# A fused attention and feed-forward kernel: one matmul chunk of the head moved, and the last store cut into two partition halves

## The chip, the cores and the metric

The kernel runs on one core of one Trainium2 chip. The metric is the device time of one execution in microseconds, as the median of repeated runs. A core has five engines that run their own instruction streams and meet at semaphores: TensorE (PE) multiplies matrices into PSUM, VectorE (DVE), ScalarE (ACT) and GpSimd (POOL) work elementwise, and SyncE (SP) issues transfers. ACT issues a few transfers too. The transfers of all of them run on the core's 16 DMA engines; in the profile, SP's queue is q1 and ACT's is q10.

## The reference

Input x is 2048 tokens of 448 features, bf16. All of it is computed on the normalised tokens:

```python
xn = layernorm(x)
# A: linear attention with 16 heads of 28 features, no softmax
q, k, v = heads(xn @ wqkv)
pq, pk = phi(q), phi(k)          # phi(t) = where(t > 0, t + 1, exp(t)) + 1e-6
kv, z = sum_s(pk * v), sum_s(pk) # per head: 28 x 28 and 28
s = merge(pq @ kv / (pq @ z + 1e-6)) @ wo
# B: feed-forward with squared ReLU, 1792 hidden features
g = silu(relu(xn @ w1 + b1) ** 2 @ w2 + b2)
out = x + s * g
```

## The kernel before, in words

The tokens stand as 16 tiles of 128, in four groups of four. The 448 features are three chunks of 128 rows and a rest of 64; the rest is held twice, in both partition halves, so that two matmuls on 64 rows each can run in the two halves of the PE array.

The kernel lists its operations in program order. A small planner (`Program.schedule`, line 89) then places them: the order on PE and SP is the order in which they are written; on ACT, DVE and POOL the planner picks by its own estimated durations and due times, and some operations may go to either of two engines. PSUM has eight banks; each new accumulator gets the bank that comes free first in the plan. For the head, the orders on ACT and DVE are written out by hand (line 1125 on). `emit` (line 232) turns the plan into instructions and waits; the last thing on SP is a wait until every store to the output has landed.

The stages, in order of PE's work:

1. The head (lines 1062 to 1146). While the first tiles load, PE runs eight warm-up matmuls. Then tiles 0 to 3 are normalised on DVE (`ln_norm`, line 486; its 1/std comes from two ACT operations, lines 477 and 481), transposed by PE against an identity matrix (`turn`, line 523), and copied back as xT by DVE or ACT. Between the transposes PE runs what already has its operands: `k0` and `k1` are the key projections of tiles 0 and 1 (line 647, 512 columns per chunk), `first[0..3]` are the first 256 columns of the hidden features h0 to h3 for tiles 0 and 1 (line 694, 256 columns per chunk). `h_mains(fi, ks)` (line 1088) issues the chunks `ks` of h`fi`; `h_mains(1)` is all three. A chunk of h0 or h1 reads the first w1 piece, a load of 192 KB, and chunk c of xT of tiles 0 and 1. `turn("T..")` names: T00 to T02 are chunks 0 to 2 of tile 0, T10 and T12 those of tile 1, T03 the rests of tiles 0 and 1, T2 and T3 the chunks of tiles 2 and 3, T23 their rests. The operation at line 1106 transposes the bias b1.
2. The streams (lines 1159 to 1187): keys, queries and hidden features of all four groups, four accumulators at a time. The transposed tiles 4 to 15 come from DMA transposes that SP issues. The hidden features 8 to 13 read the last third of w1 (`w1c`, line 464), which SP loads in three transfers.
3. Token sums, the denominator, the folding of wv and wo, and then the gates and the outputs (lines 1192 to 1233): gates `gg` are 14 matmuls over the hidden features (line 969) and a Silu on ACT; outputs `ss` are four matmuls (line 1037), a product with the gate on DVE, the residual add, and a store issued by SP.
4. The end (lines 1234 to 1243). Tile 15 goes in two column pieces, `ca` with 288 and `cb` with 160 columns. The gate of `cb` has its bias added by a matmul (line 968), so that ACT reads PSUM directly; DVE multiplies and adds the residual; the store of `ca` is issued by SP and that of `cb` by ACT.

The order of PE's instructions around the first place of the change is therefore: T00, T01, T02, k0 chunk 0, T10, k0 chunk 1, T12, k0 chunk 2, k1 chunk 0, h0 chunk 0, k1 chunks 1 and 2, b1, h0 chunks 1 and 2, T03, h1 chunks 0 to 2, T2, h2, T3, h3, T23, and then the rests.

Of the kernel before, what the change touches and what calls it, by code (L numbers as in the profile page):

```python
# [9 lines left out]
P = 128  # L10
S, D, F = 2048, 448, 1792
# [45 lines left out]
class Program:  # L57
# [8 lines left out]
    def add(self, eng, emit, reads=(), writes=(), dur=0.2, alts=(), nbytes=0):  # L66
        op = Op(eng, emit, reads, writes, dur, alts, nbytes)
        for t in op.reads:
            w = self.writer.get(t)
            if w is not None:  # L70
                op.raw.add(w)
            self.readers.setdefault(t, []).append(op)
        for t in op.writes:
            w = self.writer.get(t)
            if w is not None and w is not op:
                op.deps.add(w)
            for r in self.readers.get(t, ()):
                if r is not op:
                    op.deps.add(r)
            self.writer[t] = op  # L80
            self.readers[t] = [r for r in self.readers.get(t, ()) if r is op]
        op.raw.discard(op)
        op.deps |= op.raw
        for d in op.deps:
            d.succ.append(op)
        self.ops.append(op)
        return op
# [203 lines left out]
def bass_recurrent_scan__linear_attn_block__dense_activation_squared_relu__prompt_kernel(  # L291
# [4 lines left out]
    with ExitStack() as es:  # L296
# [44 lines left out]
        obuf = xn[:, :, :].rearrange("p s d -> p (s d)")[:, 0 : 8 * D].rearrange("p (s d) -> p s d", d=D)  # L341
# [12 lines left out]
        def bcast(ap, reps):  # L354
# [9 lines left out]
                out=ident[:, :], in_=ident[:, :], pattern=[[-1, P]], compare_op=ALU.not_equal, fill=1.0,  # L364
# [37 lines left out]
        o_r = out[0].rearrange("(p s) d -> p s d", s=NT)  # L402

        def dma(eng, dst, src, writes, nbytes, reads=()):
            return add(eng, lambda e, _: e.dma_start(dst, src), reads, writes, 0.5, nbytes=nbytes)
# [117 lines left out]
        def turn(name, si, chunks, eng, tiles=1):  # L523


            b = Buf("T")
            pieces = [(si + t, c) for t in range(tiles) for c in chunks]
            n = len(pieces)
            for i, (t, c) in enumerate(pieces):
                reads = xn_of(t)[min(c, 1) :][:1] or xn_of(t) if c < 3 else [("xd", t)]  # L530
                add(
                    "pe",
                    lambda e, _, i=i, t=t, c=c: e.transpose(  # L533
                        ps(b)[:, i * 64 : (i + 1) * 64].bitcast(bf), xn[:, t, c * P : (c + 1) * P], ident[:, :]
                    ),
                    reads + ["ident"] + ([b] if i else []), [b], 0.06,
                )

            def ev(e, _):
                src = ps(b)[:, 0 : n * 64].bitcast(bf)  # L540
                dst = xT[:, chunks[0], si * P : (si + tiles) * P]
                if len(chunks) > 1:
                    src = src.rearrange("p (c k) -> p c k", c=n)
                    dst = xT[:, chunks[0] : chunks[0] + n, si * P : (si + 1) * P]
                if eng == "dve":
                    return e.tensor_copy(dst, src)
                return e.activation(out=dst, in_=src, func=AF.Copy)

            dur = 0.06 + 0.09 * n if eng == "dve" else 0.16 + 0.11 * n
            head[name] = add(eng, ev, [b], [("xT", t, c) for t, c in pieces], dur)  # L550
# [51 lines left out]
        def mains(u, ks=K3, reads=None):  # L602


            def f(e, _):
                for k in ks:
                    last = u.mm(e, 2, k, k == 0, False)
                return last

            reads = u.reads if reads is None else reads  # L610
            add("pe", f, reads + ([u.bank] if ks[0] else []), [u.bank], len(ks) * MM(u.n))
# [376 lines left out]
        def full(u, ks=range(NF), more=[]):  # L988


            ks = list(ks)

            def f(e, _):
                for i, k in enumerate(ks):
                    last = u.mm(e, 2, k, i == 0, i == len(ks) - 1)
                return last

            add("pe", f, u.reads + more, [u.bank], len(ks) * MM(u.n))
            u.out()
# [17 lines left out]
                [("o", si % 8, c.start), ("x", si)], [("o", si % 8, c.start)], 1.1 if eng == "pool" else 0.35, alts=alts,  # L1017
            )

        def store(si, c=slice(0, D), eng="sp"):  # L1020
            dma(
                eng, o_r[:, si, c], obuf[:, si % 8, c], [("out", si, c.start)], P * (c.stop - c.start) * 2,
                [("o", si % 8, c.start)],
            )

        def ss(si, c=slice(0, D), alts=(), eng="pool", end=True):
            b = Buf("S")
            n = c.stop - c.start
            tok = slice(si * P, (si + 1) * P)
            rtok = slice(si // 2 * P, (si // 2 + 1) * P)  # L1030

            def mm(e, h, k, start, stop):
                if k < 3:
                    q, m = pqT[half[h], k, tok], msb[half[h], k, c]
                else:
                    q, m = pqR[half[h], rtok], msz[:, si % 2, c] if h == 2 else msb[half[h], 3, c]
                return e.matmul(ps(b)[:, 0:n], q, m, start=start, stop=stop)  # L1037

            def out():
                finish(si, b, c)  # L1040
                residual(si, c, eng, alts)
                if end:
                    store(si)

            return Acc(b, reads_s(si), mm, out, n)
# [42 lines left out]
        def h_mains(fi, ks=K3):  # L1088
            xs = xT_of(0) + xT_of(1)
            mains(first[fi], ks, [x for x in xs if x[2] in ks] + [("w1a", fi // 2 * 3)])  # L1090
# [9 lines left out]
        mains(k0, (2,), [("xT", 0, 2)])  # L1100
        mains(k1, (0,), [("xT", 1, 0)] + wk0)
        h_mains(0, (0,))
        mains(k1, (1, 2), [("xT", 1, 1)])
        bb = Buf("B1")
        b1v = lambda: ps(bb)[:, 0 : P // 2].bitcast(bf)
# [3 lines left out]
        )  # L1109
        h_mains(0, (1, 2))  # L1110
        turn("xT03", 0, (3,), "act", 2)
        h_mains(1)
        turn("xT2", 2, K3, "act")
        h_mains(2)
        turn("xT3", 3, K3, "dve")
# [20 lines left out]
        a, b, c, d = second  # L1136
# [99 lines left out]
        ca, cb = slice(0, 288), slice(288, D)  # L1236
        full(ss(14), KS, ["msz"])
        full(gg(15, ca))
        full(ss(15, ca, eng="dve", end=False), KS, ["msz"])
        store(15, ca)  # L1240
        full(gg(15, cb, True), range(NF + 1))
        full(ss(15, cb, eng="dve", end=False), KS, ["msz"])
        store(15, cb, "act")
        pr.schedule()
        pr.emit(nc, es)

# [27 lines left out]
```

## Time and profile before

| | |
|---|---|
| median of 16 runs | 141.27 us (140.74 to 141.93) |
| the profiled execution's own time | 141.93 us |
| its span, first to last instruction | 140.4 us |
| PE busy | 136.6 us, 97% of the span |
| DVE, ACT, POOL busy | 93.1, 78.2, 22.8 us |
| granted PE clock | 0.999 |
| DMA | 12.90 MB, 92 GB/s over the span |
| the last store: issue, size, time to landing | 138.81 us, 40 KB, 1.6 us |

In timeline rows the first two numbers are the start and the duration in us, then engine, source line, operation, output<-input, and a count; brackets hold the idle time of the engine before the row and who ended it. PEld is the weight load of a matmul, SPq and ACTq are the issues of transfers, and their durations are those of the issue, not of the transfer. Rows of waits give total, count and longest. Rows of transfers end in the KB of each and the median time from issue to landing. In DMA rows with 40 digits, each digit is the busy share, in tenths, of the 16 DMA engines in a fortieth of the window.

### The profile page before, as it was taken

What the parts mean: (1) busy time and instruction counts of PE and PEld (TensorE: products, weight loads), DVE (VectorE), ACT (ScalarE), POOL (GpSimd) and SP (SyncE); (2) the same over time, 40 slices, a digit from 0 to 9 for tenths busy, and PEclk for the clock granted to TensorE, in tenths of its full rate; (3) what the DMA queues carried; (4) which work ended last, traced back from release to release, by engine and by line L of the source; (5) the groups of instructions that cost most, each with busy time, mean ns of one, the idle gap of its engine ahead of it and who ended that gap; (6) DMA issues with size and microseconds to landing.
All of it is one profiled execution on the core that took longest, in us unless ns stands there. A gap on an engine that the chain in (4) does not pass through costs nothing.

```text
span 140.4 us, 3131 instructions
## 1 busy us (share of the span) xinstructions
PE 136.6 (97%) x1271; PEld 72.4 (52%) x1271; DVE 93.1 (66%) x227; ACT 78.2 (56%) x153; POOL 22.8 (16%) x35
## 2 busy tenths in 40 slices
PE   9899899999999999999999999999999999999993
PEld 2484355555555555555555555644555555555472
DVE  3989777898888997779896920216956062451743
ACT  4779779887988896979887922512033030200311
POOL 2710000000000000000910000000001419082680
PEclk9999999999999999999999999999999999999999
DMA  6997967999541400000000046980000102112132
GB/s 189 250 331 206 87 166 191 355 274 153 117 60 29 84 9 5 0 19 5 0 0 0 15 116 166 169 138 6 0 0 5 65 0 82 53 50 81 32 104 65
DMA packets 20353, 12.90 MB, mean 92 GB/s; under 512 B 9524, under 2 KB 19956, under 8 KB 20340
## 3 DMA queue, kind: packets, MB, share of 16 engines
q1 hardware_dynamic: 18332, 11.52, 35.1%
q10 hardware_dynamic: 2008, 1.19, 4.4%
q8 instruction: 10, 0.16, 0.5%
q14 instruction: 3, 0.02, 0.1%
HBM read 8.78 MB, written 2.10 MB: 77 GB/s over the span
## 4 chain that ended last, share of the span: by engine, by line
PE 87%; DMA 8%; DVE 2%; ACT 1%; issue 0%; ACTq 0%
PE pb L694 30%; PE pb L969 25%; PE pb L647 9%; PE pb L1037 7%; PE pb L728 7%; PE pb L678 6%; DMA xT<-tiles 6%; DMA x_tok<-in_A_x_dram 2%; PE pb L735 1%; DVE st L467 1%; PE pb L533 1%; PE pb L867 0%; ACT pqT L625 0%; DVE gbuf L980 0%; DVE xn L490 0%
## 5 line engine op out<-in xcount | busy, mean ns | idle before, releaser
L694 PE MATMUL pb<-xT,w 64*128 64x512 bf16 (+2 forms) x408 | 52.2, 365 | 0.5 <-ACT rstd L481 0.5
L969 PE MATMUL pb<-w,r 64*128 64x448 bf16 (+3 forms) x406 | 45.1, 343 | 0.1
L703 ACT ACTIVATE r<-pb,b1f 128x512 bf16<-128x512 f32 x56 | 35.1, 688 | 3.3 <-PE pb L694 3.3
L694 PEld LDWEIGHTS pb<-xT,w 64*128 64x128 bf16 (+1 forms) x408 | 25.0, 94 | 20.0 <-ACT rstd L481 1.0
L969 PEld LDWEIGHTS pb<-w,r 64*128 64x128 bf16 (+1 forms) x406 | 23.0, 95 | 20.0 <-issue 0.7
L945 ACT ACTIVATE gbuf<-gbuf 128x448 bf16<-128x448 bf16 (+1 forms) x16 | 8.8, 567 | 36.6 <-DVE gbuf L980 35.9
L980 DVE TENSOR_TENSOR gbuf<-pb,b2b 128x448 bf16<-128x448 f32 (+1 forms) x16 | 9.3, 610 | 27.7 <-PE pb L969 27.7
L1016 POOL TENSOR_TENSOR xn<-xn,x_tok 128x448 bf16<-128x448 bf16 x15 | 15.1, 1032 | 51.0 <-DVE xn L1005 51.0
L647 PE MATMUL pb<-w_qkv,xT 64*128 64x512 bf16 (+1 forms) x106 | 18.1, 377 | 0.0
L678 PE MATMUL pb<-xT,w_qkv 64*128 64x512 bf16 x84 | 15.8, 376 | 0.0
L711 DVE TENSOR_TENSOR r<-r 128x512 bf16<-128x512 bf16 x42 | 14.6, 418 | 0.9 <-ACT r L703 0.9
L394 POOL MEMSET kvm<- 128x2048 bf16 x1 | 1.8, 1805 | 59.2 <-DVE zb L672 59.2
L467 DVE BATCH_NORM_STATS2 st<-x_tok 128x6 f32<-128x448 bf16 x16 | 9.3, 612 | 3.2 <-DMA x_tok<-in_A_x_dram 3.2
L1037 PE MATMUL pb<-msb,pqT 64*128 64x448 bf16 (+3 forms) x93 | 10.9, 343 | 0.0
L635 DVE SCALAR_TENSOR_TENSOR qk<-pb,qk 128x512 bf16<-128x512 f32 x16 | 10.6, 685 | 0.2
L625 ACT ACTIVATE qk<-pb 128x512 bf16<-128x512 f32 x16 | 8.9, 595 | 3.0 <-PE pb L647 2.5
L1005 DVE TENSOR_TENSOR xn<-pb,gbuf 128x448 bf16<-128x448 f32 (+2 forms) x17 | 9.2, 591 | 1.8 <-ACT gbuf L945 1.2
L647 PEld LDWEIGHTS pb<-w_qkv,xT 64*128 64x128 bf16 (+1 forms) x106 | 7.1, 94 | 5.3
L728 PE MATMUL pb<-qk,xn 128*128 128x448 bf16 x48 | 9.3, 353 | 0.0
L625 ACT ACTIVATE pqT<-pb 128x512 bf16<-128x512 f32 x12 | 6.8, 597 | 3.3 <-PE pb L694 2.3
L678 PEld LDWEIGHTS pb<-xT,w_qkv 64*128 64x128 bf16 x84 | 6.3, 94 | 4.4
L712 ACT ACTIVATE r<-r 128x512 bf16<-128x512 bf16 x14 | 8.4, 638 | 0.0
(74 smaller groups left out, 98.3 us busy)
## 6 DMA issues: line engine op xcount, KB each, us to landing
out_dram<-xn SPq DMA_DIRECT2D x15, 112.0 KB, 1.7
w<-in_B_w_dram SPq DMA_DIRECT2D x1, 1568.0 KB, 9.6
x_tok<-in_A_x_dram SPq DMA_DIRECT2D x3, 448.0 KB, 3.9
xT<-rows ACTq DMA_DIRECT2D x6, 112.0 KB
w<-in_B_w_dram SPq DMA_DIRECT2D x1, 576.0 KB, 5.9
xT<-rows SPq DMA_DIRECT2D x5, 112.0 KB
w_o<-in_A_wo_dram SPq DMA_DIRECT2D x1, 392.0 KB, 10.7
w_qkv<-in_A_wqkv_dram SPq DMA_DIRECT2D x1, 384.0 KB, 3.9
```

The costliest lines, as they stand in the source:

```text
L467: add("dve", lambda e, _: e.bn_stats(st6[:, si, :], x_tok[:, si, :]), [("x", si)], [("st", si)], 0.58),
L625: add("act", lambda e, _: e.activation(out=slot, in_=src(), func=AF.Exp), [buf, "actw"], [tile], 0.6)
L635: lambda e, _: e.scalar_tensor_tensor(out=slot, in0=src(), scalar=1.0 + 1e-6, in1=slot, op0=ALU.add, op1=ALU.max),
L647: return e.matmul(ps(b)[:, 0:512], xT[half[h], c, si * P : (si + 1) * P], w_qkv[half[h], c, 384 : 2 * D], start=start, stop=stop,)
L678: return e.matmul(ps(b)[:, 0:512], w_qkv[half[h], c, m * P : (m + 1) * P], xT[half[h], c, g * 512 : (g + 1) * 512], start=start, stop=stop,)
L694: return e.matmul(ps(b)[:, c0 : c0 + n], w_1[half[h], c, fi * P : (fi + 1) * P], xT[half[h], c, t : t + n], start=start, stop=stop,)
L703: lambda e, _: e.activation(out=slot, in_=ps(b)[:, 0:512], func=AF.Relu, bias=b1f[:, fi : fi + 1]),
L711: return e.tensor_tensor(out=slot, in0=slot, in1=slot, op=ALU.mult)
L728: last = e.matmul(ps(b)[:, 0:D], xn[:, si, c * P : (c + 1) * P], pk_of(si), start=(si == 0), stop=(si == NT - 1),)
L969: return e.matmul(ps(b)[:, 0:n], r2[half[h], fi, si * P : (si + 1) * P], w_2[half[h], fi, c], start=start, stop=stop)
L1016: eng, lambda e, _: e.tensor_tensor(out=ob, in0=ob, in1=x_tok[:, si, c], op=ALU.add),
L1037: return e.matmul(ps(b)[:, 0:n], q, m, start=start, stop=stop)
```

## The change

In the head, h1's chunk 0 is issued right behind h0's chunk 0, ahead of chunks 1 and 2 of k1; h1's chunks 1 and 2 stay where h1 was. At the end, the store of tile 15's last 160 columns is issued as two transfers of 64 partitions each: the first half from ACT, the second from SP.

```diff
-        def store(si, c=slice(0, D), eng="sp"):
+        def store(si, c=slice(0, D), eng="sp", p=slice(0, P)):
             dma(
-                eng, o_r[:, si, c], obuf[:, si % 8, c], [("out", si, c.start)], P * (c.stop - c.start) * 2,
+                eng, o_r[p, si, c], obuf[p, si % 8, c], [("out", si, c.start, p.start)], 2 * P * (c.stop - c.start),
                 [("o", si % 8, c.start)],
             )
...
         mains(k1, (0,), [("xT", 1, 0)] + wk0)
         h_mains(0, (0,))
+        h_mains(1, (0,))
         mains(k1, (1, 2), [("xT", 1, 1)])
...
         h_mains(0, (1, 2))
         turn("xT03", 0, (3,), "act", 2)
-        h_mains(1)
+        h_mains(1, (1, 2))
         turn("xT2", 2, K3, "act")
...
         full(ss(15, cb, eng="dve", end=False), KS, ["msz"])
-        store(15, cb, "act")
+        store(15, cb, "act", slice(0, 64))
+        store(15, cb, "sp", slice(64, P))
```

## The prediction

> **What bounds the kernel now.** I read the page's busy shares and its chain first, then TensorE's waits, then the timeline at the two places that the change touches, and last the DMA traffic behind the final store.
>
> ```profile
> PE 136.6 (97%) x1271; PEld 72.4 (52%) x1271; DVE 93.1 (66%) x227; ACT 78.2 (56%) x153; POOL 22.8 (16%) x35
> ...
> PE 87%; DMA 8%; DVE 2%; ACT 1%; issue 0%; ACTq 0%
> ```
>
> ```profile
> PE pb L694 <- ACT rstd L481: 0.5, 1, 0.5
> PE pb L533 <- DVE xn L490: 0.4, 1, 0.4
> ```
>
> TensorE is the bound: 97% busy, 87% of the chain that ends last, and granted full clock in all 40 slices. Its waits over the whole span are few; the two in the second fence are all that count, 0.41 us at 4.29 before the first transpose and 0.51 us at 17.29. Between 17.29 and 137.9 it waits for nobody. So a saving ahead of 17.29 is worth something only if it gets past that 0.51 us wait, and the end is worth something only in what follows the last matmul at 137.9.
>
> The first place of the change, from the timeline at 6 to 8 us:
>
> ```profile
> 6.02 0.10 PEld L694 LDWEIGHTS pb<-xT,w 128*128 128x128 bf16 x1 [0.24 <-DMA w<-in_B_w_dram]
> 6.02 0.28 PE L694 MATMUL pb<-xT,w 128*128 128x256 bf16 x1
> ...
> 6.18 0.60 PE L647 MATMUL pb<-w_qkv,xT 128*128 128x512 bf16 x2
> ...
> 6.62 0.22 PE L1106 MATMUL pb<-ident,b1r 128*128 128x128 bf16 x1
> ...
> 7.41 0.41 DVE L490 TENSOR_SCALAR xn<-x_tok,mv,rstd 128x384 bf16<-128x384 bf16 x1
> ...
> 7.88 0.17 PEld L533 LDWEIGHTS pb<-ident,xn 128*128 128x128 bf16 x3 [0.17 <-DVE xn L490]
> ```
>
> The reader sees h0's first chunk start at 6.02, when the first w1 piece has landed, then K1's other two chunks at 6.18, and at 7.88 the transposes of tile 3, which had to wait for VectorE's normalised tile (7.41 + 0.41 = 7.82).
>
> The wait at 17.29, with the w1 loads that were issued at 9.05:
>
> ```profile
> 16.40 0.38 PE L694 MATMUL pb<-xT,w 64*128 64x512 bf16 x1
> ...
> 17.29 0.37 PE L694 MATMUL pb<-xT,w 64*128 64x512 bf16 x1 [0.51 <-ACT rstd L481]
> ```
>
> ```profile
> 9.05 1.77 SPq L405 DMA_DIRECT2D w<-in_B_w_dram  x3
> ```
>
> ```profile
> w<-in_B_w_dram SPq DMA_DIRECT2D x1, 48.0 KB, 6.9
> ```
>
> The phase at 17.29 is h8 with Q2. It reads no rstd; it is the first that reads the last third of w1 (w1c), and the third of those loads, issued at 10.22, took 6.9 us: it landed at 17.1. ACT's rstd ended at 17.18 and is only the nearest event. So this wait is on a load, whose issue at 10.22 nothing in the change moves.
>
> The second place, the end, and the two bursts of stores in it (slices of 0.04 us from 138.8):
>
> ```profile
> 137.83 0.30 ACT L945 ACTIVATE gbuf<-pb 128x160 bf16<-128x160 f32 x1 [0.59 <-PE pb L968]
> 138.10 0.33 SPq L405 DMA_DIRECT2D out_dram<-xn  x1
> 138.18 0.33 DVE L1005 TENSOR_TENSOR xn<-pb,gbuf 128x160 bf16<-128x160 f32 x1
> 138.54 0.24 DVE L1016 TENSOR_TENSOR xn<-xn,x_tok 128x160 bf16<-128x160 bf16 x1
> 138.81 0.37 ACTq L405 DMA_DIRECT2D out_dram<-xn  x1
> ```
>
> ```profile
> DMA  0003699985300000000000468965200000000000
> ...
> out_dram<-xn ACTq DMA_DIRECT2D x1, 40.0 KB, 1.6
> ```
>
> The last store is issued at 138.81 and lands 1.6 later, which is the end of the span (140.4). Of the 1.6 us, 0.84 pass before the first packet (slice 21, 139.64), 0.36 are packets (slices 21 to 29, to 140.0), and 0.4 pass after the last one. The SP store before it has the same shape: issued at 138.10, packets from slice 3 (138.92) to slice 11.
>
> **The change part by part.** The profiled execution took 141.93 us with a span of 140.4, so 1.5 us lie around the span; it is 0.66 above the median of 141.27. I add the differences below to the median.
>
> *The moved chunk.* One 128x128 weight load and one matmul of 256 columns (0.11 us each in the chain: three take 0.33) go from behind the T03 transposes to behind h0's first chunk. No matmul is added or dropped; the emitted program has one more semaphore update on TensorE, which costs nothing beside the 1271 matmuls. The chunk reads what h0's first chunk has just waited for (w1 piece 0, xT of tiles 0 and 1) and a PSUM bank that is freed by the first eviction (VectorE's copy at 4.56, 0.23 long). It issues no DMA, and no queue is passed. Before, h0's chunk feeds 0.11 us from 6.02 and K1's next starts at 6.18, so 0.05 us were open there, when ACT's eviction of K1's operand (5.74 + 0.38) ended at 6.12. So K1's chunks, the b1 transpose and T03 come 0.06 later (0.11 less 0.05), and from h1's remaining chunks on TensorE is 0.05 earlier. ScalarE takes the b1 transpose at 7.28, behind its rstd at 7.17, and T03's eviction at 7.35; T03's matmuls end at 7.16, so 0.06 later is still in time, and ScalarE afterwards idles 0.51 before 8.70 in any case. K1 is next touched at 8.60.
>
> Where does the 0.05 go? To T3: it waits for VectorE until 7.88 with or without it, and VectorE's tile does not depend on TensorE (its rstd comes from ScalarE's own chain). Were it to survive, it would go into the wait at 17.29, which takes up 0.51 us in either direction. Gain: 0.00; if both covers were gone, -0.05 to +0.06.
>
> The order on ScalarE and VectorE is made by the planner, so I checked by hand whether it can change. In the plan's own figures (they set the order; they say nothing of the chip) the T2 transposes wait for normalised tile 2, by 0.03 before; after the move TensorE gets there 0.08 earlier and waits 0.11, and T2 stands at the same planned instant. The head's ScalarE order is fixed by hand. TensorE's summed due times from there on are the same, and the three PSUM banks only swap names. So the plan from T2 on should be the old one: 0.00.
>
> *The split store.* Removed: one ACT issue of 128 rows (0.37). Added: an ACT issue and an SP issue of 64 rows of 320 bytes. SP ended its previous issue at 138.43 and now waits for VectorE's last add until 138.78, as ACT does; behind it on SP there is only the wait for all stores, and nothing else waits for SP. That final wait now needs both halves.
>
> Nothing in the trace stores 64 rows alone, so I bound it. *Issue:* alone 0.33 on SP and 0.37 on ACT; the one pair of plain 128-row transfers that SP and ACT issue close together, at the start, took 0.39 on both. I take +0.04, the mean of the two increases. *Packets:* half the rows each; if they ran side by side, 0.18 instead of 0.36, so -0.18. *First packet of the later half:* the same pair bears on it:
>
> ```profile
> 0.00 0.39 SPq L405 DMA_DIRECT2D x_tok<-in_A_x_dram  x1
> ...
> 0.16 0.39 ACTq L405 DMA_DIRECT2D x_tok<-in_A_x_dram  x1
> ```
>
> ```profile
> DMA  0000000903989921916199916906933143347135
> ...
> q1 hardware_dynamic: 67, 0.06, 65.0%
> ```
>
> The second fence is the DMA view from 0.90 to 1.56. Only SP's queue (q1) moves there, from 1.02 on; ACT's packets (q10) come only after 1.56, so 1.40 after their issue instead of 0.84: 0.56 late. SP's own came 1.02 after issue against 0.82 to 0.84, so 0.2 of the lateness is the start's own, and 0.36 is the wait behind 128 rows of the other queue. Behind 64 rows that is 0.18. The further row is the pair at 81.4, where ACT's first packet came 1.36 after its issue (81.41 to 82.77, again with q1 alone ahead of it): 0.52 late. I take 0.18, from the nearer row, plain row transfers.
>
> Sum: +0.04 - 0.18 + 0.18 = +0.04. Lower end: no lateness, no longer issue, and the landing a little shorter for fewer bytes (1.7 for 112 KB, 1.6 for 40 KB, so 0.03 for another 20 KB): -0.18 - 0.03 = -0.21. Upper end: 0.52 late, +0.04, and packets no quicker, because both halves share the engines: +0.56.
>
> A rule speaks against this half of the change. The Trainium skill, page "DMA: Bandwidth & Descriptors", section "Rules for kernel authors", says not to bother with two transfers to disjoint partition halves, since both spread over the same 16 DMA engines and serialize. The pair at the start agrees with it (q10 silent until q1's first transfer is through). By that rule the packets would gain nothing and the later half would only pay the longer issue, so the sum would be +0.04, the same as mine.
>
> Forecast: 141.27 + 0.00 + 0.04 = 141.31.
>
> **The rivals.** *Slower: the halves hold each other up.* Place: between 138.81 and the first packet of the later half. For: both concurrent pairs in the trace show it, 0.56 and 0.52 late. Against: half the rows, and no loads in flight as at the start. Price +0.56, so 141.83. It decides, against 0.28 us (0.2%), once the later half's first packet is more than 0.24 late with packets not shortened, or 0.42 with them halved.
>
> *Faster: the halves run side by side, and the moved chunk's 0.05 gets through.* For: 0.36 us of packets at the end hide behind nothing, and the profile names ACT, not a load, for the wait at 17.29; if that were right, ACT's work would shift with TensorE. Against: the w1c landing at 17.1, the wait at 7.88, both concurrent pairs. Price: -0.21 - 0.05 = -0.26, so 141.01: about the bound, and past it only with the scatter of a median.
>
> *The plan changes.* Then ScalarE and VectorE take evictions in another order somewhere after 8 us. Against: the resynchronisation at T2 worked out above. TensorE has no waits after 17.29, so there is little to gain; one eviction in the wrong place costs up to its own 0.69 us (VectorE's phi step, 0.685 mean), 141.96 at most.
>
> **How the numbers follow.** 0.2% is 0.28 us, about what a measurement of this kernel tells from no change. No change that can be seen: 0.60. The halves hold each other up: 0.25. Side by side with the chunk's gain: 0.11. A changed plan: 0.04, nearly all slower. Faster needs the third and some scatter, so 0.11; slower 0.29 from the second and fourth. The likeliest is 141.31, by itself 141.05 to 141.55. The range takes in the lower and upper ends of the unknown store: 141.0 (141.27 - 0.26) to 141.85 (141.27 + 0.56, rounded up).
>
> **What the profile after would show.** Right: h1's first chunk at about 6.13 and K1's chunks at 6.24; T3 still at 7.88 behind the normalised tile; a wait of 0.5 to 0.6 before h8 at 17.29; at the end ACT and SP issues within 0.05 us of each other, and landing 1.5 to 1.75 after. Wrong: TensorE at a time other than 17.29 there, w1c landing elsewhere, new waits of TensorE after it, or a first packet of the later half past 1.1 us from its issue. What would make the forecast wrong above all is the price of two queues started at one instant, which the trace has only for larger and different transfers.

## The result, and the profile after

The changed kernel takes 141.72 us (median of 9 runs, 141.41 to 141.96; a tenth on record, 142.26, is not among them) against 141.19 for the kernel before (48 runs): the ratio is 1.0035, with a 95% interval of 1.0022 to 1.0047. That is 0.5 us slower. It lies inside the range of the prediction, but on the side of its first rival and beyond 0.2%; the likeliest value, 141.31, was 0.4 too low.

The page of the kernel after, busy shares and chain, and below it TensorE's waits:

```profile
PE 136.3 (97%) x1271; PEld 72.7 (52%) x1271; DVE 92.9 (66%) x227; ACT 78.2 (56%) x153; POOL 22.8 (16%) x35
...
PE 95%; DVE 2%; DMA 2%; ACT 0%; issue 0%
```

```profile
PE pb L533 <- DVE xn L490: 0.4, 1, 0.4
PE pb L1078 <- DVE ones L358: 0.3, 1, 0.3
```

The wait of 0.5 us before h8 is gone, and the span of this execution is 139.9 us, shorter than the 140.4 of before, although the kernel is slower. So one must not subtract these two spans. The execution profiled before was the slowest of the runs shown (141.93 against a median of 141.27); experiment 3 below shows what the kernel before looks like otherwise.

The head, from the timeline after:

```profile
5.86 0.12 PEld L694 LDWEIGHTS pb<-xT,w 128*128 128x128 bf16 x2 [0.18 <-DMA w<-in_B_w_dram]
5.88 0.38 PE L694 MATMUL pb<-xT,w 128*128 128x256 bf16 x2
...
6.10 0.59 PE L647 MATMUL pb<-w_qkv,xT 128*128 128x512 bf16 x2
...
7.32 0.42 DVE L490 TENSOR_SCALAR xn<-x_tok,mv,rstd 128x384 bf16<-128x384 bf16 x1
...
7.79 0.17 PEld L533 LDWEIGHTS pb<-ident,xn 128*128 128x128 bf16 x3 [0.28 <-DVE xn L490]
```

The two chunks of h0 and h1 now run as a pair from 5.88, and K1's chunks follow at 6.10. At tile 3's transposes TensorE arrives earlier, and there it waits longer: 0.28 us in place of 0.17. The transposes start when VectorE's tile is there (7.32 + 0.42 = 7.74), as in the profile before.

The end, from the timeline, and the DMA view from 137.7 to 139.7 in slices of 0.05 us:

```profile
137.13 0.33 DVE L1005 TENSOR_TENSOR xn<-pb,gbuf 128x160 bf16<-128x160 f32 x1
137.49 0.24 DVE L1016 TENSOR_TENSOR xn<-xn,x_tok 128x160 bf16<-128x160 bf16 x1
137.76 0.53 SPq L405 DMA_DIRECT2D out_dram<-xn  x1
137.76 0.55 ACTq L405 DMA_DIRECT2D out_dram<-xn  x1
```

```profile
DMA  0001689963100000000000001376303574200000
GB/s 0 0 0 46 196 265 334 334 196 81 23 0 0 0 0 0 0 0 0 0 0 0 0 0 26 64 128 116 64 13 58 96 135 84 39 0 0 0 0 0
...
q1 hardware_dynamic: 224, 0.09, 17.9%
q10 hardware_dynamic: 80, 0.02, 5.6%
issues: line engine op xcount, KB each, median us to landing
out_dram<-xn SPq DMA_DIRECT2D x1, 20.0 KB, 1.8
out_dram<-xn ACTq DMA_DIRECT2D x1, 20.0 KB, 2.1
```

Both halves are issued at the same instant, 0.03 after the add ends, so SP waits no longer than ACT. But each issue takes 0.53 or 0.55 where one of 128 rows took 0.37, and the first burst in the right half of the row starts only in slice 24 (138.9). There are two bursts with a dip between them at slice 29 (139.15): SP's half first, then ACT's. ACT's half lands 2.1 us after its issue; the whole store of before landed in 1.6. By the landing events in the trace it is 2.09 against 1.57, so 0.52 more, which is the measured loss of 0.5 within its interval.

### The profile page after: what moved, and what is told of

It reads as the page before. It is cut to its first block, busy times and chain, and to the rows that moved or that the text cites. A ratio compares the mean times of both kernels' runs of the same rounds, so it can differ in the third digit from the quotient of the medians.

```text
span 139.9 us, 3132 instructions
## 1 busy us (share of the span) xinstructions
PE 136.3 (97%) x1271; PEld 72.7 (52%) x1271; DVE 92.9 (66%) x227; ACT 78.2 (56%) x153; POOL 22.8 (16%) x35
## 4 chain that ended last, share of the span: by engine, by line
PE 95%; DVE 2%; DMA 2%; ACT 0%; issue 0%
PE pb L969 30%; PE pb L694 30%; PE pb L647 9%; PE pb L1037 8%; PE pb L728 7%; PE pb L678 6%; DMA x_tok<-in_A_x_dram 2%; PE pb L735 1%; PE pb L533 1%; DVE st L467 1%; PE pb L829 1%; PE pb L790 1%; PE pb L867 0%; DVE xn L490 0%; DVE mv L468 0%; DVE xn L1005 0%
## 5 line engine op out<-in xcount | busy, mean ns | idle before, releaser
L666 DVE TENSOR_TENSOR zacc<-zacc,qk 128x448 f32<-128x448 f32 x13 | 8.1, 623 | 0.3
```

## The experiments

The ratios and their intervals stand as recorded; a ratio is not the quotient of the two medians and can differ from it by 0.1%. Wherever only some rows are stored, `store` has the argument `p` of the change; its lines are not repeated below.

**1. The head alone.** The last store stays whole and on ACT.

```diff
         h_mains(0, (0,))
+        h_mains(1, (0,))
         mains(k1, (1, 2), [("xT", 1, 1)])
...
-        h_mains(1)
+        h_mains(1, (1, 2))
```

> Only the head's part of the change: h1's first chunk behind h0's first chunk; the last store whole, from ACT, as before. Theory 1 (all of the loss is in the two halves of the last store, the moved chunk is worth nothing): 141.2, ratio 1.000 within 0.001, the last store landing 1.57 us after its issue; h8's phase starts when the third w1c load has landed, or without a wait where that load is early, in before and here alike. Theory 2 (the moved chunk costs): ratio about 1.003, and TensorE's matmuls after 8 us later than in before at equal load landings. Theory 3 (the moved chunk takes the wait before h8 away, as the profile after has none there, and the store loses more than the sum shows): ratio 0.997 to 0.999 and no wait before h8.

Measured: 141.0 us against 141.12, ratio 0.9996, interval 0.9979 to 1.0013. The last store landed 1.57 after its issue. So the moved chunk is worth nothing that can be measured; the interval leaves room for 0.3 us of gain or 0.2 of loss. In this execution the w1 piece that h0's first chunk reads came late, and TensorE waited for it before h0. Tile 3's transposes, the last row, then found VectorE's tile just done (7.65 + 0.38 = 8.03) and no wait:

```profile
6.43 0.11 PEld L694 LDWEIGHTS pb<-xT,w 128*128 128x128 bf16 x2 [0.75 <-DMA w<-in_B_w_dram]
...
7.65 0.38 DVE L490 TENSOR_SCALAR xn<-x_tok,mv,rstd 128x384 bf16<-128x384 bf16 x1
...
8.09 0.26 PEld L533 LDWEIGHTS pb<-ident,xn 128*128 128x128 bf16 x3
```

The length of the wait before h0 differs from one execution to the next (0.75 on the weight load here, 0.24 in the first profile of the kernel before, 0.18 after), as the landing of the loads does.

**2. The split store alone.** The head is as before.

```diff
-        store(15, cb, "act")
+        store(15, cb, "act", slice(0, 64))
+        store(15, cb, "sp", slice(64, P))
```

> Only the last store's part of the change: 64 partitions from ACT, 64 from SP; the head as before. Theory 1: the same as the whole change, ratio 1.0035 (141.7); both issues take 0.53 to 0.55 us, the later half's first packet comes about 1.45 after its issue, and it lands 2.1 after. Theory 2: ratio within 0.001 of 1. Theory 3: ratio above 1.0045.

Measured: 141.73 us against 141.12, ratio 1.004, interval 1.0021 to 1.006; issues of 0.53 and 0.55, landings of 1.83 (SP) and 2.09 (ACT). This part alone gives the whole loss within the intervals. Theory 1 stands as to the place, theory 2 falls.

**3. The kernel before, a second profile.** No edit.

> The kernel before, unchanged, for a second profile. It tells whether the wait of 0.5 us before h8 and the third w1c load's landing at 17.1 belong to the kernel or to the one execution profiled. Theory 1: ratio 1.000 within 0.001; the w1c load may land anywhere between 14.8 (profile after) and 17.1 (profile before), and where it lands before 16.4 there is no wait. Theory 3: the wait is there again, since the moved chunk is what removes it.

Measured: ratio 1.0004, interval 0.9988 to 1.002, which is the scatter of an unchanged kernel. TensorE's waits in it, and the second and third of the w1c loads:

```profile
PE pb L533 <- DVE xn L490: 0.6, 1, 0.6
PE pb L1078 <- DVE ones L358: 0.3, 1, 0.3
```

```profile
w<-in_B_w_dram SPq DMA_DIRECT2D x2, 48.0 KB, 5.4
```

There is no wait before h8: the same load takes 5.3 us here and lands at 15.5 instead of 17.1. TensorE starts h8 at 16.80, 0.49 before the first profile's 17.29, and its last matmul 0.80 before, with no change at all. So the wait at 17.29 belonged to one execution, and theory 3 falls: the moved chunk didn't remove it. That it was the load shows in the trace: TensorE's own wait instruction for the second and third w1c loads stands from 16.79 to 17.12 in the first profile, and takes 0.05 in the second. The other 0.30 come at 97.76, where in the first profile TensorE stood behind VectorE, which had waited for the replicated rows (97.09 + 0.62 = 97.71):

```profile
96.88 0.29 DVE L936 TENSOR_TENSOR pqR<-pqR,xT 128x256 bf16<-128x256 bf16 x1 [0.35 <-DMA xT<-tiles]
97.09 0.62 DVE L980 TENSOR_TENSOR gbuf<-pb,b2b 128x448 bf16<-128x448 f32 x1
```

**4. Two column halves at the same instant.** Each transfer has all 128 partitions and 80 columns.

```diff
-        store(15, cb, "act")
+        for c, eng in ((slice(288, 368), "act"), (slice(368, D), "sp")):
+            dma(eng, o_r[:, 15, c], obuf[:, 7, c], [("out", 15, c.start)], 2 * P * 80, [("o", 7, 288)])
```

> The last store as two transfers of all 128 partitions and 80 columns each, ACT and SP at the same instant; the head as before. If the price is that two queues are started at once, whatever they carry: issues of 0.53 to 0.55, the later first packet 1.45 or more after its issue, and, with 128 rows in each, a landing past 2.1: ratio 1.0035 to 1.006. If the price came from 64 rows being moved slowly (fewer rows per DMA engine), 128 rows would move at the old pace: landing 1.6 to 1.75, ratio 1.000 to 1.0015.

Measured: 141.39 us against 141.12, ratio 1.001, interval 0.9994 to 1.0026. The DMA view from 138 to 140:

```profile
DMA  0001699963000000005888762000000000000000
...
out_dram<-xn SPq DMA_DIRECT2D x1, 20.0 KB, 1.5
out_dram<-xn ACTq DMA_DIRECT2D x1, 20.0 KB, 1.7
```

The issues took 0.33 and 0.38. One burst holds both halves: by the trace's packets, SP's start 0.83 after its issue and ACT's 0.91 after its own, and they run at the same time. Same queues, same instant, the same bytes, and twice the rows of the halves by partitions, but nearly the old landing. So two queues started at once, whatever they carry, are not the price. What is different is the count of 64 partitions, with rows of 320 bytes instead of 160.

**5 and 6. 64 rows alone, 32 rows alone.** Only one transfer, from ACT; the other rows of the last piece aren't stored. Each was executed once, for its profile.

```diff
-        store(15, cb, "act")
+        store(15, cb, "act", slice(0, 64))     # experiment 5
+        store(15, cb, "act", slice(0, 32))     # experiment 6
```

> The head as before. Of the last 160 columns of tile 15 only partitions 0 to 63 are stored, from ACT; the other 64 rows of that piece are left out, so nothing is issued beside it. Theory A (a transfer of 64 partitions is itself dearer to issue and slower to start than one of 128): issue 0.53 to 0.55 although it is alone, first packet about 1.15 after the issue, landing about 1.8. Theory B (64 rows are cheap alone; two at once hold each other up, more than two of 128 rows did): issue 0.37, first packet 0.86, landing 1.45 to 1.55.

> As the run with 64 rows alone, with partitions 0 to 31 of the last piece only (the other 96 rows of it are left out). If the issue's price is one of any count below 128: 0.53 to 0.55 again, with a landing a little under that of 64 rows. If it grows as rows fall: over 0.6. Theory B: 0.37 and a landing of 1.4 to 1.5.

Timeline and transfer rows, 64 rows alone:

```profile
137.93 0.53 ACTq L405 DMA_DIRECT2D out_dram<-xn  x1
```

```profile
DMA  0005799741000000000000002564100000000000
...
out_dram<-xn ACTq DMA_DIRECT2D x1, 20.0 KB, 1.8
```

32 rows alone:

```profile
137.77 0.34 ACTq L405 DMA_DIRECT2D out_dram<-xn  x1
```

```profile
out_dram<-xn ACTq DMA_DIRECT2D x1, 10.0 KB, 1.4
```

With nothing beside it, half of the rows takes longer than the whole: an issue of 0.53 and a landing of 1.84 for 64 rows, against 0.37 and 1.57 for 128 rows. But 32 rows take 0.34 and 1.42. The halves that had nothing ahead of them agree: SP's in the profile after, and the first in experiment 7, also took 0.53 to issue and 1.8 to land. So this part of the price is neither the company nor the smallness: of these counts, 64 is the dear one. Theory A holds for 64 rows and not for every count under 128. Company costs too, as theory B has it, for the later half: 2.09 beside the other half against 1.84 alone.

**7 and 8. Both halves on SP, and the whole piece on SP.**

```diff
-        store(15, cb, "act")
+        store(15, cb, "sp", slice(0, 64))      # experiment 7, two lines
+        store(15, cb, "sp", slice(64, P))
...
+        store(15, cb, "sp")                    # experiment 8
```

> The last piece as two stores of 64 partitions, both from SP, one after the other; the head as before. Theory A: each issue 0.50 to 0.60; the second is issued 0.55 after the first and lands 1.7 to 1.8 after its own issue, 2.3 after the first's: ratio 1.004 to 1.006. Theory B: issues of 0.33, the second landing 0.35 + 1.5 = 1.85 after the first issue: ratio 1.001 to 1.003.

> The last piece whole, as before, but issued by SP in place of ACT. Both theories: issue 0.33, landing 1.53 to 1.61, ratio 0.999 to 1.001. It is the base for the two halves on SP, and tells whether SP's own place in the end matters.

Measured for the halves: 142.17 us against 141.06, ratio 1.0076, interval 1.0048 to 1.0104; issues of 0.53 and 0.60, and the second lands 2.47 after the first is issued. Theory A expected 2.3; the ratio came out above the range written for it, with its interval reaching into it. For the whole: ratio 0.999, interval 0.9975 to 1.0004, issue 0.33, landing 1.54. SP is as good a place as ACT for it, and no half on it is.

**9 and 11. Cuts at other rows.** 96 partitions from ACT and 32 from SP; then 80 and 48 (this one for its profile only).

```diff
-        store(15, cb, "act")
+        store(15, cb, "act", slice(0, 96))     # 80 in experiment 11
+        store(15, cb, "sp", slice(96, P))      # 80 in experiment 11
```

> The last piece in two partition parts at the same instant as in the change, but cut 96 (ACT) and 32 (SP) in place of 64 and 64; the head as before. If it is the count of 64 that is dear: the 32 rows issue in 0.34 and land about 1.42 to 1.5 after, the 96 rows issue in 0.35 to 0.40 and land 1.55 to 1.7, ratio 0.9995 to 1.0015. If any cut by partitions is dear, and 32 rows were cheap only because nothing ran beside them: landing of the later part at 1.9 to 2.1, ratio 1.0025 to 1.004.

> The last piece cut 80 (ACT) and 48 (SP) partitions, issued at the same instant; the head as before. It tells whether 64 is alone in being dear. If only 64 is: issues of 0.33 to 0.39 and landings of 1.42 to 1.66 for both. If counts near 64 are dear too: an issue of 0.5 or more on the part concerned and a landing of 1.8 or more.

The issues of 96 and 32 with the DMA view from 137.6 to 139.6, then the transfer rows of 96 and 32, and those of 80 and 48:

```profile
137.69 0.35 SPq L405 DMA_DIRECT2D out_dram<-xn  x1
137.69 0.38 ACTq L405 DMA_DIRECT2D out_dram<-xn  x1
```

```profile
DMA  0000378995200000001569864000000000000000
```

```profile
out_dram<-xn ACTq DMA_DIRECT2D x1, 30.0 KB, 1.6
out_dram<-xn SPq DMA_DIRECT2D x1, 10.0 KB, 1.4
```

```profile
out_dram<-xn ACTq DMA_DIRECT2D x1, 25.0 KB, 1.7
out_dram<-xn SPq DMA_DIRECT2D x1, 15.0 KB, 1.5
```

For 96 and 32 the ratio is 1.0012, interval 0.9997 to 1.0026; one time of 80 and 48 was 141.04 against 141.06. In these two uneven cuts the parts are issued in 0.35 and 0.38, both move in one burst, and the later one lands in 1.63 to 1.67. A cut by partitions isn't dear as such; 64 and 64 is. Nor does such a cut gain anything: 1.63 is still above the 1.57 of the whole.

**10. The moved chunk with the whole piece on SP**, the best of what the runs offered: the diff of experiment 1 and the line of experiment 8.

> The moved chunk with the last piece stored whole by SP: the version that the runs so far make the best one of. The moved chunk measured 0.9996 and the whole store on SP 0.999, both with 1 inside the interval; the landing of the last store was 1.535 on SP against 1.57 on ACT. If these are real: ratio 0.998 to 0.9995. If they are scatter: 1.000 within 0.001.

Measured: 140.9 us against 141.12, ratio 0.9987, interval 0.9974 to 0.9999. It is the only version with an interval wholly below 1, but by less than the 0.2% that a measurement of this kernel tells from no change; with nine ratios measured, one such interval doesn't show a gain.

## Why the prediction was right or wrong

**The moved chunk: the price right, its reason in part.** It was put at 0.00, because tile 3's transposes wait for VectorE. Experiment 1 measured 0.9996, and the profile after shows a longer wait there (0.28 in place of 0.17). But that wait is no property of the kernel either. With the old order it is 0.16 or 0.17 in six of the ten profiles and under 0.1 in the other four; with the new one it is 0.28, 0.20 (experiment 10) and none (experiment 1). So the time gained ahead of it is not well known (0.03 to 0.11 by these rows, against the 0.05 that I had read off), and where the wait is absent, nothing at tile 3 holds the gain back. The measurement can't tell so little from nothing: that the price is small is shown, that the wait swallows all of it is not. The order did hold: VectorE's instructions stand in the same order in both kernels, and ScalarE's differ only in the shape of the last store.

**The wait at 17.29: the cause right, its standing wrong.** The profile after has the third w1c load land in 4.5 us in place of 6.9, and no wait, while ScalarE's rstd still ends at 17.13, after h8 has begun. So it was the load and not rstd. But I took one execution's landing for a property of the kernel. In a second profile of the same kernel the wait was absent, so that cover of 0.51 us was not to be counted on. That the profiled run lay 0.66 above the median was the warning. Nor did TensorE wait for nobody between 17.29 and 137.9: it lost 0.30 at 97.76 in the same profile (experiment 3), behind a transfer that the chain's 8% for the DMA pointed at.

**The split store: the wrong terms.** The prediction had issue +0.04, packets -0.18 and first packet of the later half +0.18, a sum of +0.04. For the later half, by the trace's issue, packets and landing in the profiles before and after:

| from issue to landing, us | before, 128 rows | 64 rows alone | after, later half |
|---|---|---|---|
| issue | 0.37 | 0.53 | 0.55 |
| end of issue to first packet | 0.50 | 0.66 | 0.90 |
| first to last packet's end | 0.31 | 0.26 | 0.26 |
| last packet to landing | 0.39 | 0.39 | 0.38 |
| sum | 1.57 | 1.84 | 2.09 |

So the issue term was +0.18, not +0.04; the packets gained 0.05, not 0.18; and between the end of the issue and the first packet the later half lost another 0.40. From issue to first packet that is 0.59 more (1.45 against 0.86), where the prediction had 0.18 and a longer issue of 0.04. The 0.31 is the trace's time for the packets of before; the 0.36 of the prediction was read off slices. The column in the middle separates the two causes: 0.27 of the 0.52 is the price of 64 rows with nobody beside them, and 0.25 comes with the other half, whose last packet ended at 139.209 while ACT's first started at 139.212. In experiment 2 the same two instants are 139.201 and 139.206.

The failing step is the one that took two transfers of 128 rows as the nearest row for two of 64. I had noted that the trace has no store of 64 rows alone, and scaled: half the rows, half the wait. The row itself was also misread. The prediction says that ACT's queue is silent until SP's first transfer is through. But a transfer of 128 rows is 144 packets, and only 67 of SP's had moved when ACT's began at 1.56; from there to 2.2, in the DMA view of the kernel before, the two queues ran side by side:

```profile
q10 hardware_dynamic: 139, 0.11, 51.0%
q1 hardware_dynamic: 101, 0.08, 45.4%
```

So the start showed an overlap, as experiment 4 did later, and no wait for the end of the other transfer that could be halved. The trace did have 64-row loads, the twins of the rest rows. Here is the first of them, in the timeline of the kernel before, with the load ahead of it:

```profile
1.92 0.49 SPq L405 DMA_DIRECT2D w<-in_B_w_dram  x1
2.45 0.56 SPq L405 DMA_DIRECT2D w_qkv<-in_A_wqkv_dram  x1
```

A load of 64 KB on 64 partitions took longer to issue than one of 192 KB on 128. All ten of these 64-row loads in the first 11 us took 0.50 to 0.60, against 0.33 to 0.37 for nearly all of the 128-row stores. But the 128-row loads of the same stretch took anything from 0.39 to 0.59, so these rows would not have settled it; they would have put the issue term's upper end at +0.2.

**The rivals.** The first, that the halves hold each other up, had the right sign and nearly the right price (0.56 against 0.52). Its mechanism was half right: there is a wait beside the other half, 0.25, but of the cuts tried only between two transfers of 64 rows. Column halves overlapped, and so did 96 with 32. The rest of the loss, 0.27 for 64 rows that are dear by themselves, was in neither the sum nor a rival. So it is partly luck that the range held: its upper end, +0.56, is the lateness of another pair (0.52) with no gain in packets, and the measured 0.59 to the first packet less 0.05 in the packets came just below it. The prediction's own signs of being wrong did show: h8 started at 16.55 and not at 17.29, the third w1c load landed at 14.8, and the later half's first packet came 1.45 after its issue, past the 1.1. The second and third rival did not occur. The Trainium skill's rule of the page "DMA: Bandwidth & Descriptors", section "Rules for kernel authors", that partition halves serialize, agrees with the two bursts of the profile after; the sum that I made from it, +0.04, was too small all the same, since 64 rows cost more alone than 128. The rule speaks of halves; two parts of 96 and 32 or of 80 and 48 rows overlapped here, and still gained nothing.

**What stays open.** Why 64 rows are dear. The runs tell that of the counts tried only this one is (32, 48, 80, 96 and 128 are not; 48, 80 and 96 in one profile each), and that it lies in the issue and in what comes between it and the first packet (0.16 each) and not in the packets. They do not tell what does it, why two such transfers don't overlap, or whether stores of 64 rows of another length behave so. The trace's 64-row loads were issued among others, so they bound the issue alone.

## What to carry to other kernels

Most of the last store's time here was issue, start and receipt; a cut in two can shorten only the packets, which were 0.31 of 1.57 us, and no cut that was tried landed earlier than the whole. Before cutting a transfer into equal halves by partitions, look in the trace for how long transfers with that count of rows take to issue, and try an unequal cut or one by columns. And take a second profile before counting a wait as a cover, above all where the profiled run lies well above the median: the 0.5 us that looked like one here was a late load of one execution, and the 0.17 us at tile 3 was absent in others.

## What the runs showed of the hardware

A store of 64 partitions x 320 bytes took 1.84 us from issue to landing and 0.53 to issue, while 128 partitions took 1.57 and 0.37, and 32 partitions 1.42 and 0.34, all alone on ACT's queue. Two stores issued on SP and ACT within 0.01 us of each other overlapped in the DMA engines when they had 128 rows each, 96 and 32, or 80 and 48 (later landing 1.63 to 1.67), but went one after the other when they had 64 each (2.09). Landing times of the same load in the same kernel differed by 1.6 us between two executions (5.3 and 6.9 us for the 48 KB of w1c).
